# Retention and a routed MoE on one core: full-array transposes, whole-token products and state sums a step ahead

## The chip, the cores and the metric

The kernel runs on one core of a Trainium2 chip. Its time is the device time of one launch in microseconds (us); the time before is the median of three runs. Engines are named as in the profile: PE is TensorE's matmuls, PEld its weight loads, DVE is VectorE, ACT ScalarE, POOL GpSimd, and SP SyncE, which only issues DMAs here. Lines such as L354 are lines of the kernel before.

## The reference

A retention layer makes 3072 tokens of 512 numbers, and each token then goes through the one of eight experts that its logits choose.

```python
for t in range(S):                       # q, k, v: (4, 8, 768, 64)
    state = gamma * state + k[t] (x) v[t]          # per batch and head, 64x64
    y[t] = scale * q[t] @ state
x = y.transpose(0, 2, 1, 3).reshape(3072, 512)
logits = x @ w_gate;  e = argmax(logits)           # 8 experts
gate_w = softmax(logits)[e];  eom = sigmoid(x @ w_output_gate)[e]
out = gate_w * eom * (relu(x @ w1[e]) @ w2[e])     # w1: 512x1024, w2: 1024x512
```

## The kernel before

**Retention.** Each batch of 768 tokens is worked in chunks of 128, two chunks a step: twelve steps j (NP), three a batch. All eight heads go together, as four groups g of two (NG). Every product is a quarter of the PE array, 64x64, so that four independent products can stand in it. A step turns the queries and keys by products with the identity (`turn_q` L279 and `turn_k` L296, 32 products each, copied out of PSUM by ACT as qt and kt), makes the scores within blocks of 64 tokens (`scores`, 32), masks them on DVE (`masked`, am), multiplies them with the scaled values vs (`group`, into py), adds the keys' and values' products to the running state in the PSUM tile st (`group` also, alternating with the former), copies that state out four times (sx, L362) and reads it with the queries (`read`, L371, into py again, closed by a one-column DVE copy "seen", L378). DVE scales py into yt (L382). `tokens` (L394) turns yt back to tokens by products with idw, which holds the identity and the two gate matrices side by side, so that the logits come out with the tokens; ACT copies the result as xr (L398).

**Routing, two steps later.** `route1` and `gate` on DVE find the expert (oh, ef) and the gate value gt, `rows` (L449) multiplies the tokens by gt into rows, `count` (L460) counts tokens per expert on PE, `route2` works out each token's place, and `scatter` sends rows to the array srt in DRAM by POOL.

**Order.** The stage is scheduled by hand: every engine runs its instructions as the code calls them, in line. PSUM pairs 0, 1 and 2 (`pair(n)`) are passed from hand to hand, `free` says which is empty. SP loads three steps ahead (`load(j + 3)`) and brings the first weights in the last steps (`w_at`; `s_at` splits them into a high and a low part, whi and wlo, on ACT, DVE and POOL).

**Head and MoE.** The expert with most tokens after the fifth step (`choose`, pick, read into an SP register by values_load) gets its first 256 rows worked in the tail of the retention stage, as "head": stage 1, relu on ACT, the low part on DVE (L572), stage 2, transposes ot. Its products are handed out piece by piece by `run_head(n)`. After the last scatter DVE ranks the experts, pads srt, and works out n_odd, the number of rows that need the rare path. Then eight MoE passes: `load_x` (L805) on SP brings sorted rows, `prep_x` transposes and splits them (xt, xh L823, xw), stage 1 (L836), hh and hl (L840, L841), stage 2 (L855). The last pass turns its output by twelve full transposes (L881).

Of the kernel before, what the change touches and what calls it, by code (L numbers as in the profile page):

```python
# [31 lines left out]
def retention_moe_kernel(  # L32
# [157 lines left out]
    with ExitStack() as actx:  # L190
# [40 lines left out]
        gv = ac.tile([P, NC, H], F32, name="gv")  # L231
        gq = ac.tile([P, NPB, 2, 2, NG, 64], F32, name="gq")
        gc = ac.tile([P, NC, 2, NG], F32, name="gc")
        idw = ac.tile([P, NG, 2, 64 + 2 * E], F32, name="idw")
# [3 lines left out]
        for u in range(2):  # L238
            for r in range(2):
                h = r ^ u  # L240
                nc.scalar.dma_start(
                    gq[half(r), 0, u, 0],
                    dec_q[h:h + 1].rearrange("o (g t) -> o g t", g=NG)[:, :, half(u)].broadcast_to([64, NG, 64]))
        for u in range(2):
            for r in range(2):
                h = r ^ u
                nc.scalar.dma_start(gc[half(r), :, u],
                                    dec_c[h:h + 1].rearrange("o (c g) -> o c g", g=NG).broadcast_to([64, NC, NG]))
        load(1)
        for x, w in enumerate((w_gate, w_ogate)):  # L250
            wv = w.rearrange("(g r f) e -> r f g e", r=2, f=64)
            for u in range(2):
                for r in range(2):
                    nc.sync.dma_start(idw[half(r), :, u, 64 + x * E:64 + x * E + E], wv[r ^ u])
        load(2)

        def gq_rest(jj):
            for w in range(2):
                if jj or w:
                    nc.gpsimd.tensor_mul(gq[:, jj, :, w], gq[:, 0, :, 0],  # L260
                                         gc[:, 2 * jj + w].unsqueeze(3).broadcast_to([P, 2, NG, 64]))

        def prep_v(j):
            c = 2 * (j % NPB)
            vs[j] = ap.tile([P, 2, H, D], F32, name="vs", tag="vs", bufs=2)
# [3 lines left out]
        def mm64(out, o, ro, lhs, rhs, start=True, stop=True):  # L269
            nc.tensor.matmul(out, lhs, rhs, start=start, stop=stop, skip_group_check=True)  # L270

        def turn_q(j, n):
            p = pt["q", j] = pair(n, "pq")
            pv = p.rearrange("p w (g r m) -> p w g r m", g=NG, r=2)
            for g in range(NG):
                for r in range(2):
                    for w in range(2):
                        for hh in range(2):
                            nc.tensor.matmul(pv[half(hh), w, g, r], qn[j][half(w), 2 * g + hh, r], ident[half(w), half(w)],  # L279
                                             start=True, stop=True, skip_group_check=True)  # L280

        def copy_q(j):
            t = qt[j] = ap.tile([P, 2, NG, P], F32, name="qt", tag="qt", bufs=2)
            nc.scalar.copy(t.rearrange("p w g (m r) -> p (w g) r m", r=2),
                           pt.pop(("q", j)).rearrange("p w (g r m) -> p (w g) r m", g=NG, r=2))
            qn.pop(j)

        def turn_k(j, n, ws):
            if 0 in ws:
                pt["k", j] = pair(n, "pk")  # L290
            pv = pt["k", j].rearrange("p u (w g s) -> p u w g s", w=2, g=NG)
            for w in ws:
                for g in range(NG):
                    for u in range(2):
                        for hh in range(2):
                            nc.tensor.matmul(pv[half(hh), u, w, g], kn[j][half(u), w, 2 * g + hh], ident[half(u), half(u)],  # L296
                                             start=True, stop=True, skip_group_check=True)

        def copy_k(j):
            t = kt[j] = ap.tile([P, 2, 2, NG, 64], F32, name="kt", tag="kt", bufs=2)  # L300
            nc.scalar.copy(t.rearrange("p u w g s -> p (u w g s)"), pt.pop(("k", j)).rearrange("p u x -> p (u x)"))

        def scores(j, n):
            p = pt["s", j] = pair(n, "sc")
            pv = p.rearrange("p hh (w g t) -> p hh w g t", w=2, g=NG)
            for w in (1, 0):
                for g in range(NG):
                    for hh in range(2):
                        for u in range(2):
                            nc.tensor.matmul(pv[half(u), hh, w, g], kt[j][half(hh), u, w, g], qt[j][half(hh), w, g, half(u)],  # L310
                                             start=True, stop=True, skip_group_check=True)
            kt.pop(j)

        def masked(j):
            pv = pt.pop(("s", j)).rearrange("p hh (w g t) -> p hh w g t", w=2, g=NG)
            for w in range(2):
                a = am[j, w] = ap.tile([P, 2, NG, 64], F32, name="am", tag="am", bufs=2)
# [14 lines left out]
        def values(j, n):  # L332
            pt["y", j] = (pair(n, "py"), set())

        def group(j, w, u):

            c = 2 * (j % NPB) + w
            py = newest(j)
            x = 1 - u
            st_ops, av_ops = [], []  # L340
            for g in range(NG):
                for hh in range(2):
                    if not (c == NC - 1 and u == 1):
                        st_ops.append((st[half(hh), g], kn[j][half(u), w, 2 * g + hh], vs[j][half(u), w, 2 * g + hh],
                                       c == 0 and u == 0 and g == 0))
                    r = hh
                    h = r ^ x
                    av_ops.append((py[half(r), x, w, g], vs[j][half(x), w, 2 * g + h], am[j, w][half(x), h, g],
                                   begins(j, x, r)))
            for n in range(2 * NG):  # L350
                for ops in (av_ops, st_ops):
                    if ops:
                        o, l, m, s = ops[n]
                        nc.tensor.matmul(o, l, m, start=s, stop=True, skip_group_check=True)  # L354

        def copy_s(j, w, u):
# [3 lines left out]
            if j < NP and not (j % NPB == 0 and w == 0 and u == 0):  # L360
                t = sx[j, w, u] = ap.tile([P, NG, 64], F32, name="sx", tag="sx", bufs=6)
                nc.scalar.copy(t, st)  # L362

        def read(j, w):
            py = newest(j)
            for g in range(NG):
                for hh in range(2):
                    for r in range(2):
                        u = hh ^ r
                        if (j, w, u) in sx:  # L370
                            nc.tensor.matmul(py[half(r), u, w, g], sx[j, w, u][half(hh), g], qt[j][half(hh), w, g, half(u)],  # L371
                                             start=begins(j, u, r), stop=True, skip_group_check=True)
            first = (j, w, 0) not in sx
            sx.pop((j, w, 0), None), sx.pop((j, w, 1), None)
            if first:
                return
            t = sm.tile([P, 1], F32, name="seen", tag="seen")
            nc.vector.tensor_copy(t, py[:, 0, w, NG - 1, 63:64])  # L378

        def copy_y(j):  # L380
            t = yt[j] = ap.tile([P, 2, 2, NG, 64], F32, name="yt", tag="yt", bufs=2)
            nc.vector.tensor_tensor(out=t.rearrange("p u w g t -> p (u w g t)"), in0=pt.pop(("y", j))[0].rearrange("p u x -> p (u x)"),  # L382
                                    in1=gq[:, j % NPB].rearrange("p u w g t -> p (u w g t)"), op=ALU.mult)
            kn.pop(j), vs.pop(j), qt.pop(j), am.pop((j, 0)), am.pop((j, 1))

        X = 64 + 2 * E

        def tokens(j, w, n):
            p = pair(n, "px")
            pv = p[:, :, 0:NG * X].rearrange("p hh (g x) -> p hh g x", g=NG)  # L390
            for g in range(NG):
                for r in range(2):
                    for u in range(2):
                        nc.tensor.matmul(pv[half(u), r ^ u, g], yt[j][half(r), u, w, g], idw[half(r), g, u],  # L394
                                         start=True, stop=True, skip_group_check=True)
            if w == 0:
                xr[j] = ap.tile([P, 2, 2, NG, X], F32, name="xr", tag="xr", bufs=2)
            nc.scalar.copy(xr[j][:, w].rearrange("p hh g x -> p hh (g x)"), p[:, :, 0:NG * X])  # L398
            if w == 1:
                yt.pop(j)  # L400

        def route1(j):
            x8 = xr[j].rearrange("p w hh g x -> p w (hh g) x")
# [651 lines left out]
```

## Time and profile before

| | |
|---|---|
| median of three runs | 540.55 us (538.72 to 542.15) |
| profiled execution | 538.24 us, of it the span 536.5 us |
| PE busy | 427.9 us, 80% of the span |
| DVE, ACT, POOL busy | 265.5, 182.1, 172.1 us |
| mean granted clock of PE | 0.903 |
| prologue, loop of twelve steps | to about 24 us, to about 200 us |
| tail with head and ranking | to about 251 us |
| MoE passes | to the end |

The span is the profiled program on its engines; 1.74 us of the execution's time lie around it. Busy shares are means over stages that are held by different things: the MoE passes keep PE full, the loop does not. [...]

### The profile page before, as it was taken

The numbers are of one execution on the slowest core, as the hardware profiler recorded it, in microseconds if no ns is written. First come the engines' busy times: TensorE is split into PE (matmuls) and PEld (weight loads), VectorE is DVE, ScalarE is ACT, GpSimd is POOL, SyncE is SP. The second block draws the span as 40 slices with busy tenths as digits, with TensorE's granted clock in tenths as the row PEclk, the third lists the DMA queues.
The fourth block names the chain that finished last, engine by engine and source line by source line (L and its number), as shares of the span: only waits on it lengthen the run. The fifth ranks groups of instructions, "written<-read, shape, count | busy, mean of one in ns | idle before, by whom it ended". The sixth has DMA issues, their size and how long they took to land.

```text
span 536.5 us, 16878 instructions
## 1 busy us (share of the span) xinstructions
PE 427.9 (80%) x7027; PEld 409.1 (76%) x7027; DVE 265.5 (49%) x756; ACT 182.1 (34%) x356; POOL 172.1 (32%) x215
## 2 busy tenths in 40 slices
PE   5267676866777546493699999999999999999993
PEld 3256565766666545493699999999999999999992
DVE  1012354565456775714645745754756557566211
ACT  2023332333225442111344433533534444444111
POOL 0325122333334553300232203424424344242442
PEclk9588688798789977796889999999999999999998
DMA  6669996518811442105657538448467484563001
GB/s 123 137 122 222 209 248 162 123 44 213 226 43 50 125 152 81 61 22 157 120 177 204 150 107 198 143 129 216 146 166 193 147 210 149 157 183 96 30 27 60
DMA packets 130072, 74.16 MB, mean 138 GB/s; under 512 B 60213, under 2 KB 118585, under 8 KB 129984
## 3 DMA queue, kind: packets, MB, share of 16 engines
q1 hardware_dynamic: 121872, 59.43, 43.8%
q0 software_dynamic: 5280, 13.23, 7.2%
q8 instruction: 57, 0.93, 0.8%
q10 hardware_dynamic: 2832, 0.31, 0.5%
q14 instruction: 31, 0.25, 0.1%
HBM read 59.73 MB, written 13.70 MB: 137 GB/s over the span
## 4 chain that ended last, share of the span: by engine, by line
PE 64%; issue 13%; DVE 7%; SPq 5%; DMA 4%; POOL 3%; ACT 2%; ACTq 0%; POOLq 0%; DVEq 0%
PE a L855 21%; PE h L836 21%; PE py L354 4%; SPq L228 3%; PE pk L296 3%; POOL out_dram L177 3%; PE h L567 2%; PE sc L310 2%; PE px L394 2%; PE pq L279 2%; PE py L371 2%; PE st L354 2%; PE a L583 2%; DMA xl<-srt 2%; DVE wlo L172 2%
## 5 line engine op out<-in xcount | busy, mean ns | idle before, releaser
L177 POOL DMA_INDIRECT out_dram<-ot,idi x84 | 83.2, 991 | 155.9 <-ACT hh L840 126.1
L836 PE MATMUL h<-xh,whi 128*128 128x224 f32 (+7 forms) x256 | 87.0, 340 | 8.6 <-ACT xh L823 8.6
L855 PE MATMUL a<-hh,whi 128*128 128x224 f32 (+7 forms) x256 | 86.7, 339 | 4.3 <-ACT hh L840 4.3
L836 PE MATMUL h<-xw,whi 128*128 128x224 f32 (+7 forms) x256 | 87.0, 340 | 0.0
L836 PE MATMUL h<-xh,wlo 128*128 128x224 f32 (+7 forms) x256 | 86.8, 339 | 0.0
L855 PE MATMUL a<-hl,whi 128*128 128x224 f32 (+7 forms) x256 | 86.6, 338 | 0.1
L855 PE MATMUL a<-hh,wlo 128*128 128x224 f32 (+7 forms) x256 | 86.3, 337 | 0.0
L172 DVE TENSOR_TENSOR wlo<-raw,whi 128x512 fp32r<-128x512 f32 x64 | 47.4, 745 | 57.6 <-ACT whi L170 54.5
L841 DVE SCALAR_TENSOR_TENSOR hl<-h,hh 128x224 fp32r<-128x224 f32 (+7 forms) x64 | 34.9, 546 | 62.0 <-ACT hh L840 61.9
L170 ACT CAST whi<-raw 128x512 fp32r<-128x512 f32 x64 | 39.7, 620 | 63.9 <-PE a L855 62.4
L840 ACT ACTIVATE hh<-h 128x224 fp32r<-128x224 f32 (+7 forms) x64 | 31.0, 485 | 82.3 <-PE h L836 82.3
L836 PEld LDWEIGHTS h<-xh,whi 128*128 128x128 f32 x256 | 49.7, 194 | 9.0 <-ACT xh L823 8.8
L362 ACT COPY sx<-st 128x256 f32<-128x256 f32 x44 | 16.4, 372 | 113.4 <-PE st L354 113.4
L855 PEld LDWEIGHTS a<-hh,whi 128*128 128x128 f32 x256 | 49.0, 191 | 4.9 <-ACT hh L840 4.5
L491 POOL DMA_INDIRECT srt<-row,posi x24 | 24.1, 1005 | 82.9 <-DVE acc L485 63.5
L836 PEld LDWEIGHTS h<-xw,whi 128*128 128x128 f32 x256 | 49.6, 194 | 0.5
L836 PEld LDWEIGHTS h<-xh,wlo 128*128 128x128 f32 x256 | 49.6, 194 | 0.2
L855 PEld LDWEIGHTS a<-hl,whi 128*128 128x128 f32 x256 | 49.0, 191 | 0.8 <-DVE hl L841 0.4
L855 PEld LDWEIGHTS a<-hh,wlo 128*128 128x128 f32 x256 | 48.9, 191 | 0.5
L354 PE MATMUL py<-am,vs 64*64 64x64 f32 x768 | 41.4, 251 | 9.5 <-DVE seen L378 6.1
L354 PE MATMUL st<-vs,kn 64*64 64x64 f32 x704 | 38.3, 251 | 11.1 <-issue 11.1
L354 PEld LDWEIGHTS py<-am,vs 64*64 64x64 f32 x768 | 34.0, 159 | 12.8 <-DVE seen L378 8.1
(169 smaller groups left out, 706.1 us busy)
## 6 DMA issues: line engine op xcount, KB each, us to landing
raw<-in_moe_w_dram SPq DMA_DIRECT2D x128, 256.0 KB, 3.0
qn<-in_q_dram SPq DMA_DIRECT2D x12, 512.0 KB, 6.4
kn<-in_k_dram SPq DMA_DIRECT2D x24, 256.0 KB, 6.3
vn<-in_v_dram SPq DMA_DIRECT2D x24, 256.0 KB, 5.7
xl<-srt SPq DMA_DIRECT2D x12, 211.2 KB, 4.7
xl<-srt SPq DMA_DIRECT2D x12, 195.0 KB, 4.8
out_dram<-ot,idi POOLq DMA_INDIRECT x84, 2.7
xl<-srt SPq DMA_DIRECT2D x4, 227.5 KB, 7.4
```

What stands on the lines that cost most here:

```text
L170: nc.scalar.copy(hi[:, 0], raw[:, 0])
L172: nc.vector.tensor_sub(lo[:, 0], raw[:, 0], hi[:, 0].bitcast(F32))
L177: st = nc.gpsimd.indirect_dma_start(out=dst, out_offset=bass.IndirectOffsetOnAxis(ap=idx, axis=0), in_=src, in_offset=None, bounds_check=n ...
L228: nc.sync.dma_start(t[:, w], chunks(src, j)[:, w * P:(w + 1) * P].rearrange("h p d -> p h d"))
L296: nc.tensor.matmul(pv[half(hh), u, w, g], kn[j][half(u), w, 2 * g + hh], ident[half(u), half(u)], start=True, stop=True, skip_group_check= ...
L354: nc.tensor.matmul(o, l, m, start=s, stop=True, skip_group_check=True)
L362: nc.scalar.copy(t, st)
L491: ins = nc.gpsimd.indirect_dma_start(out=srt, out_offset=bass.IndirectOffsetOnAxis(ap=idx, axis=0), in_=src, in_offset=None, bounds_check= ...
L836: nc.tensor.matmul(ps[:, 0:C], l[:, 0, w], r[:, dc, 0:C], start=(n == 0), stop=(n == 3 * NDC - 1))
L840: relu = nc.scalar.activation(hh, ps[:, 0:C], AF.Relu)
L841: nc.vector.scalar_tensor_tensor(out=hl, in0=ps[:, 0:C], scalar=0.0, in1=hh.bitcast(F32), op0=ALU.max, op1=ALU.subtract)
L855: mm = nc.tensor.matmul(accs[d][:, 0:C], l[:, 1, w], r, start=(f == 0 and n == 0), stop=(f == NF - 1 and n == 2))
```

## The change

**Turns.** Keys and queries are turned by eight full 128x128 transposes each, two heads at a time, in place of 32 quarter products. For the queries DVE first separates even and odd tokens (`split_q`). **Outputs.** In odd groups the two heads' halves of py are swapped (`swap`), so that one product of 128x144 a group and chunk turns yt back and makes the logits: eight a step in place of 32. idw, gq and the decay factors are laid out for that; gq is prepared from gb and gc, and gab is loaded in rows of 24 numbers where gc was loaded four numbers at a time. **Order.** Turns are two steps ahead, the state sums one (`sums(j + 1, ...)`), alternating with values or scores through `issue`. **Engines.** The rows go from DVE to ACT, the seen copies go, the head's PSUM pair is another, the read of pick moves to step 7, and the rest of the head is called behind n_odd.

```diff
+                nc.scalar.dma_start(gab[half(r), x].rearrange("p c g -> p (c g)"),
+                                    dec_c[r ^ x:(r ^ x) + 1].broadcast_to([64, NC * NG]))
...
+        def split_q(j):
+            t = ap.tile([P, 2, H, D], F32, name="qr", tag="qr", bufs=1)
+            nc.vector.tensor_copy(t.rearrange("p r h d -> p h r d"), qn[j])
+            qn[j] = t
...
         def turn_q(j, n):
             p = pt["q", j] = pair(n, "pq")
+            for r in range(2):
                 for g in range(NG):
+                    nc.tensor.transpose(p[:, r, g * P:(g + 1) * P],
+                                        qn[j][:, r, 2 * g:2 * g + 2].rearrange("p h d -> p (h d)"), ident)
...
+        def turn_k(j, n):
+            p = pt["k", j] = pair(n, "pk")
+            for w in range(2):
+                for g in range(NG):
+                    nc.tensor.transpose(p[:, w, g * P:(g + 1) * P],
+                                        kn[j][:, w, 2 * g:2 * g + 2].rearrange("p h d -> p (h d)"), ident)
...
+        def issue(*lists):
+
+            for n in range(max(len(x) for x in lists)):
+                for x in lists:
+                    for o, l, m, s in x[n:n + 1]:
+                        nc.tensor.matmul(o, l, m, start=s, stop=True, skip_group_check=True)
...
+        def sums(j, w, u):
 
             c = 2 * (j % NPB) + w
+            if j >= NP or (c == NC - 1 and u == 1):
+                return []
+            return [(st[half(hh), g], kn[j][half(u), w, 2 * g + hh], vs[j][half(u), w, 2 * g + hh], c == 0 and u == 0 and g == 0)
+                    for g in range(NG) for hh in range(2)]
...
+        def tokens(j, n):
             p = pair(n, "px")
+            m = rt["misc", j] = ps_1.tile([P, 512], F32, name="misc", tag="misc")
+            for w in range(2):
+                for g in range(NG):
+                    nc.tensor.matmul(p[:, w, g * X:(g + 1) * X] if g < NG - 1 else m[:, w * X:(w + 1) * X],
+                                     yt[j][:, w, g].rearrange("p u t -> p (u t)"), idw[:, g], start=True, stop=True,
+                                     skip_group_check=True)
...
+        def copy_x(j):
+            xr[j] = ap.tile([P, 2, NG, X], F32, name="xr", tag="xr", bufs=2)
+            nc.scalar.copy(xr[j][:, :, 0:NG - 1].rearrange("p w g x -> p w (g x)"), pt.pop(("x", j))[:, :, 0:(NG - 1) * X])
+            nc.scalar.copy(xr[j][:, :, NG - 1], rt["misc", j][:, 0:2 * X].rearrange("p (w x) -> p w x", w=2))
...
-                    nc.vector.tensor_scalar(
...
+                    nc.scalar.activation(
...
+                        AF.Copy, scale=gt[:, w:w + 1])
...
+        w_at = {7: (0,), 8: (1,), 9: (2, 3), 10: (4, 5), 11: (6,)}
+        s_at = {8: (0,), 9: (1,), 10: (2, 3), 11: (4, 5)}
...
+            new_y(j, 0)
+            av = {(w, u): values(j, w, u) for w, u in ((0, 1), (1, 1), (1, 0), (0, 0))}
+            issue(av[0, 1], sums(j + 1, 0, 0))
+            copy_s(j + 1, 0, 1)
             if more:
+                split_q(j + 2)
             if j >= 2:
                 route1(j - 2)
+            issue(av[1, 0], av[1, 1])
+            issue(read(j, 0, 0), read(j, 1, 1))
+            issue(av[0, 0], sums(j + 1, 0, 1))
+            copy_s(j + 1, 1, 0)
+            if j >= 2:
                 gate(j - 2)
+                rows(j - 2)
+                count(j - 2, j - 2 in (PICK, EARLY))
             if more:
+                turn_k(j + 2, 1)
+                copy_k(j + 2)
+                turn_q(j + 2, 2)
+                copy_q(j + 2, 0)
...
+            sc = scores(j + 1, 1) if j + 1 < NP else [[], []]
+            issue(sums(j + 1, 1, 0), sc[1][0:8])
+            copy_s(j + 1, 1, 1)
+            if more:
+                copy_q(j + 2, 1)
...
+            issue(read(j, 0, 1), read(j, 1, 0))
             copy_y(j)
+            issue(sc[0][0:8], sc[1][8:16])
+            issue(sc[0][8:16], sums(j + 1, 1, 1))
+            copy_s(j + 1, 2, 0)
...
+            if j >= 1:
+                tokens(j - 1, 2)
+                copy_x(j - 1)
...
-        run_head(1000)
...
         nc.vector.tensor_add(n_odd, no, late)
+        run_head(1000)
```

The order of PE's instructions at the end of a step of the loop, before (py values and reads, st sums, px tokens, sc scores, pq the queries' turn; a row is a run of products):

```order
L354 MATMUL py<-am,vs 64x64
L354 MATMUL st<-vs,kn 64x64
L394 MATMUL px<-idw,yt 64x80 x16
L371 MATMUL py<-qt,sx 64x64 x16
L354 MATMUL py<-am,vs 64x64 x8
L310 MATMUL sc<-qt,kt 64x64 x32
L279 MATMUL pq<-ident,qn 64x64 x32
```

After, in the middle of a step, from the count to the first sums and scores of the next pair:

```order
L460 LDWEIGHTS tri_b
L460 MATMUL misc<-oh,tri_b 128x16
L461 LDWEIGHTS ones_b
L461 MATMUL misc<-acc,ones_b 128x16
L301 MATMUL pk<-ident,kn 128x128 x8
L286 MATMUL pq<-ident,qr 128x128 x8
L313 MATMUL st<-vs,kn 64x64
L313 MATMUL sc<-qt,kt 64x64
```

The turns are eight rows of 128x128 each behind the count, and scores alternate with sums in the place of standing alone.

ACT's instructions of one step before (ex and ez belong to the routing, xr are token copies, kt and qt the turned keys and queries):

```order
L415 ACTIVATE ex<-d_1513 128x16
L431 ACTIVATE ez<-z 128x2
L398 COPY xr<-px 128x640
L362 COPY sx<-st 128x256 x2
L301 COPY kt<-pk 128x1024
L398 COPY xr<-px 128x640
L362 COPY sx<-st 128x256 x2
L284 COPY qt<-pq 128x8x2x64
```

And after:

```order
L415 ACTIVATE ex<-d_1483 128x16
L368 COPY sx<-st 128x256
L431 ACTIVATE ez<-z 128x2
L449 ACTIVATE row<-xr,gt 128x2x128 x4
L306 COPY kt<-pk 128x1024
L292 COPY qt<-pq 128x512
L368 COPY sx<-st 128x256
L292 COPY qt<-pq 128x512
L368 COPY sx<-st 128x256
L400 COPY xr<-px 128x2x432
L401 COPY xr<-misc 128x2x144
```

Four rows stand between ez and the key copy, and both token copies come at the end of the step.

DVE in the tail, before, from the head's last two low parts to the first rows of the MoE stage is L572, four transposes L598, the chain L770 to L780 that ends in n_odd, and then idi. After, it is:

```order
L805 TENSOR_TENSOR no<-no,on 128x1
L806 TENSOR_TENSOR n_odd<-no,late 128x1
L574 SCALAR_TENSOR_TENSOR h_3727<-h_3105,h_3727 128x256
L574 SCALAR_TENSOR_TENSOR h_3754<-h_3105,h_3754 128x256
L844 CAST idi<-xl 128x7
L849 STREAM_TRANSPOSE xt<-xl 128x224 x2
L574 SCALAR_TENSOR_TENSOR h_3781<-h_3105,h_3781 128x256
L851 TENSOR_TENSOR xw<-xt,xh 128x224 x2
```

n_odd now stands ahead of the head's last low parts (h), and the rows' preparing (idi, xt, xw) stands between them.

## Rows read from the trace of the kernel before

**Rows 1.** Windows: length, busy us per engine (instructions), granted clock, DMA share, GB/s.
```profile
37.40:200.00 162.60, 110.84 (x4648) 100.79 (x4648) 83.66 (x353) 57.36 (x116) 56.63 (x86) 0.83 0.61 153
51.40:69.20 17.80, 12.61 (x451) 11.45 (x443) 7.28 (x33) 4.39 (x9) 6.15 (x33) 0.66 0.98 213
63.50:64.00 0.50, 0.50 (x28) 0.50 (x24) 0.43 (x5) 0.00 (x0) 0.00 (x0) 0.50 0.69 157
117.00:118.00 1.00, 1.00 (x64) 1.00 (x65) 0.86 (x4) 0.69 (x1) 0.00 (x0) 1.00 0.00 0
250.74:272.30 21.56, 17.11 (x101) 16.41 (x102) 12.01 (x26) 7.92 (x18) 4.18 (x4) 0.74 0.68 159
272.30:488.00 215.70, 215.70 (x1214) 213.70 (x1214) 127.58 (x230) 93.50 (x176) 74.85 (x76) 1.00 0.60 168
```

**Rows 2.** Waits of PE, 24 to 205 us: total, times, longest.
```profile
PE st L354 <- issue: 11.1, 5, 3.2
PE px L394 <- issue: 8.9, 5, 2.8
PE py L354 <- DVE seen L378: 6.1, 13, 1.8
```

**Rows 3.** Windows inside the loop, columns as in the first group.
```profile
105.90:109.40 3.50, 2.44 (x128) 2.18 (x128) 0.90 (x7) 1.53 (x3) 0.09 (x1) 1.00 0.02 5
109.40:112.90 3.50, 2.64 (x127) 2.36 (x128) 1.38 (x2) 0.82 (x2) 3.18 (x3) 1.00 0.41 156
...
sum 18.30, PE 12.81 PEld 11.61 DVE 10.01 ACT 7.31 POOL 6.89; mean PE 2.56 PEld 2.32 DVE 2.00 ACT 1.46 POOL 1.38
```

**Rows 4.** DMA queues, 105.9 to 124.2 us: packets, MB, share of 16 engines.
```profile
q8 instruction: 5, 0.08, 1.9%
```

**Rows 5.** Groups by line, 0 to 260 us: busy us, mean ns of one.
```profile
L398 ACT COPY xr<-px 128x640 f32<-128x640 f32 x24 | 16.7, 697 | 11.9 <-PE px L394 11.9
L362 ACT COPY sx<-st 128x256 f32<-128x256 f32 x44 | 16.4, 372 | 113.4 <-PE st L354 113.4
L449 DVE TENSOR_SCALAR row<-xr,gt 128x256 f32<-128x256 f32 x48 | 13.7, 350 | 0.2
L301 ACT COPY kt<-pk 128x1024 f32<-128x1024 f32 x12 | 12.2, 1017 | 0.0
L172 DVE TENSOR_TENSOR wlo<-raw,whi 128x512 fp32r<-128x512 f32 x9 | 9.7, 1106 | 4.2 <-ACT whi L170 4.2
L431 ACT ACTIVATE ez<-z 128x2 f32<-128x2 f32 x12 | 2.4, 203 | 3.9 <-DVE z L429 3.9
```

**Rows 6.** Timeline of PE near the end: start, us, instruction.
```profile
526.20 1.20 PE L881 MATMUL po<-ident,otl 128*128 128x128 f32 x9 [0.25 <-DVE otl L870]
```

**Rows 7.** Timeline of DVE, 198 to 205.4 us.
```profile
198.80 1.22 DVE L382 TENSOR_TENSOR yt<-py,gq 128x1024 f32<-128x1024 f32 x1 [0.78 <-PE py L354]
...
202.47 0.57 DVE L405 TENSOR_REDUCE lg<-xr 128x32 f32<-128x256 f32 x1
...
204.45 0.17 DVE L429 TENSOR_REDUCE z<-j 128x2 f32<-128x16 f32 x1
...
205.00 0.16 DVE L436 SCALAR_TENSOR_TENSOR den<-ez,se 128x2 f32<-128x2 f32 x1
205.20 0.17 DVE L438 RECIPROCAL gt<-den 128x2 f32<-128x2 f32 x1
```

**Rows 8.** DMA issues, 9 to 22 us: KB each, median us to landing.
```profile
kn<-in_k_dram SPq DMA_DIRECT2D x2, 256.0 KB, 15.1
```

**Rows 9.** The same of the whole page.
```profile
kn<-in_k_dram SPq DMA_DIRECT2D x24, 256.0 KB, 6.3
```

**Rows 10.** Waits of SP, 198 to 300 us.
```profile
SPq L805 <- DVE n_odd L780: 12.1, 1, 12.1
```

**Rows 11.** Waits of PE, 198 to 300 us.
```profile
PE h L836 <- ACT xh L823: 8.6, 1, 8.6
PE a L855 <- ACT hh L840: 4.3, 1, 4.3
```

More of the change, by code (lines that the diff above doesn't have):

```diff
@@ L272, in turn_q @@
         def turn_q(j, n):
             p = pt["q", j] = pair(n, "pq")
[L274 to L292, printed above, removed]
-                for g in range(NG):
[L294 to L297, printed above, removed]
@@ L303, in scores, with every @@
+        def issue(*lists):
[3 more added lines that the diff above has]
+                        nc.tensor.matmul(o, l, m, start=s, stop=True, skip_group_check=True)
+        def every(a, b):
+            return [x for ab in zip(a, b) for x in ab]
         def scores(j, n):
@@ L305, in scores @@
             pv = p.rearrange("p hh (w g t) -> p hh w g t", w=2, g=NG)
[L306 to L312, printed above, removed]
+            return [[(pv[half(u), hh, w, g], kt[j][half(hh), w, g, half(u)],
+                      qt[j][half(hh), g, w * P + 64 * u:w * P + 64 * u + 64], True)
+                     for w in range(2) for g in range(NG) for u in range(2)] for hh in range(2)]
         def masked(j):
@@ L330, in begins, with new_y, values @@
             return new
-        def values(j, n):
+        def new_y(j, n):
             pt["y", j] = (pair(n, "py"), set())
-        def group(j, w, u):
+        def sums(j, w, u):
             c = 2 * (j % NPB) + w
-            py = newest(j)
[L339 to L354, printed above, removed]
+            if j >= NP or (c == NC - 1 and u == 1):
+                return []
+            return [(st[half(hh), g], kn[j][half(u), w, 2 * g + hh], vs[j][half(u), w, 2 * g + hh], c == 0 and u == 0 and g == 0)
+                    for g in range(NG) for hh in range(2)]
+        def values(j, w, u):
+            py = newest(j)
+            return [(py[half(hh ^ swap(g)), u, w, g], vs[j][half(u), w, 2 * g + hh], am[j, w][half(u), hh, g],
+                     begins(j, u, hh ^ swap(g)))
+                    for g in range(NG) for hh in range(2)]
         def copy_s(j, w, u):
@@ L360, in copy_s, with read @@
             if j < NP and not (j % NPB == 0 and w == 0 and u == 0):
-                t = sx[j, w, u] = ap.tile([P, NG, 64], F32, name="sx", tag="sx", bufs=6)
+                t = sx[j, w, u] = ap.tile([P, NG, 64], F32, name="sx", tag="sx", bufs=9)
                 nc.scalar.copy(t, st)
-        def read(j, w):
+        def read(j, hh, u):
             py = newest(j)
[L366 to L378, printed above, removed]
+            return [(py[half(hh ^ swap(g)), u, w, g], sx[j, w, u][half(hh), g],
+                     qt[j][half(hh), g, w * P + 64 * u:w * P + 64 * u + 64], begins(j, u, hh ^ swap(g)))
+                    for w in range(2) if (j, w, u) in sx for g in range(NG)]
```

202 lines of the change are left out of this document (99 added, 103 removed).

## The prediction

> **What bounds the kernel now.** I read the stages by windows first, then TensorE's waits in the loop, then short windows inside a step. From 37.4 us on, where the second step begins, to the last y of the loop at 198.80 [rows 7] eleven steps take (198.8 - 37.4) / 11 = 14.7 us each. TensorE is busy for only 110.84 of 162.60 us of that stretch, at a mean granted clock of 0.83; DVE, the next, for 83.66 [rows 1]. The reader should look at what ends TensorE's waits: the longest are "issue", 11.1 us ahead of the state sums and 8.9 ahead of the token products; the wait for the vector engine's "seen" copy is 6.1 [rows 2]. "Issue" is no semaphore, so neither an engine nor a transfer is named. The short windows show what it is. With the clock at 1.00 and transfers nearly idle, TensorE takes 127 or 128 product records and as many weight-load records in 3.50 us, stops, and does so again; over one stretch it is 3.50, 3.50, 3.90, 3.80 and 3.60 us, mean 3.66, with 2.44 to 2.64 us of work in each (two of the five stand in [rows 3]). In the same 18.3 us the queue that carries instructions moved five packets, 0.08 MB [rows 4]: five blocks of 16 KB, one for each 256 records. So one block comes every 3.66 us, and **the loop is held by the supply of TensorE's instructions**, not by its arithmetic. A step's 224 quarter products are two passes each, 448 product and 448 load records, four a product, 896 in all: 3.5 blocks, 12.8 us at 3.66, near the 14.7 that a step takes; the rest is the lower clock and the waits for other engines.
>
> [...]
>
> **Fewer instructions.** A step after has 128 quarter products (sums 32, values 32, state reads 32, scores 32) at four records each, 512; sixteen full transposes, one product record and one load each (twelve transposes of the last pass are twelve records: nine of them stand in [rows 6]), 32; eight token products of two passes, 32; and four for the count: 580, or 2.27 blocks. That is 8.3 us at 3.66 a block. In the slowest stretch, 51.4 to 69.2, 451 product records took 17.80 us [rows 1], waits and a clock of 0.66 included: 5.05 us for each 128, which gives 11.5. Since 8.3 to 11.5 lies below 14.7 in any case, the question is what is late next.
>
> **The chain that is late next.** The order keeps every engine in line, and ACT now has the rows ahead of the key copy. So a step has this ring: token products, copy of them on ACT, routing and gate on DVE, rows on ACT, key copy on ACT, the scores on TensorE (they take the PSUM pair from which the keys are copied, and so wait for that copy), and the next token products. The pieces:
> - token products, a shape that the trace does not have. The nearest row is nine transposes in 1.20 us, 0.133 each [rows 6]; eight products of two passes at 0.133 are 2.1 us. At half the clock they would be 4.2. I take 2.1.
> - copy of the tokens in two parts: the 256-wide copy is 372 ns, the 640-wide 697 [rows 5], so 0.85 ns an element and 0.16 to begin; 864 and 288 wide give 0.89 + 0.40 = 1.3.
> - routing and gate: 202.47 to 205.37 in the tail, where nothing else holds them, 2.9 [rows 7].
> - four rows: 350 ns each on DVE; on ACT as the 372 ns copy of the same size [rows 5], 1.5.
> - key copy: 1.0 [rows 5].
> - sums, scores and reads behind it: 64 products, 128 records. At clock 1.00 TensorE takes 64 records in 1.00 us, at 0.50 it takes 28 in half a us [rows 1]: 2.0 us, or 2.3 at half.
> - crossings between engines: z ends at 204.62, den begins at 205.00, and between them lies only ACT's ez of 203 ns [rows 5, 7]: 0.09 a crossing, eight of them 0.7.
>
> Sum: 2.1 + 1.3 + 2.9 + 1.5 + 1.0 + 2.0 + 0.7 = **11.5 us** a step, above the supply's 8.3. TensorE's other work (half the quarter products, 2.0, the transposes, 16 x 0.133 = 2.1, the count) lies beside the 6.7 us in which the ring is on ACT and DVE; if that cover goes, 4 us come in. The clock stood at 0.83 over the loop [rows 1]; that is two thirds of the time at 1.00 and one at 0.50, and a third of the 2.4 us that half the clock adds (4.2 + 2.3 in place of 2.1 + 2.0) is 0.8. I take 12.0, of 12.3; 10.5 as the low end (part of the ring overlapped, 1.0) and 14.0 with half the clock throughout (the transposes' longer time still fits beside the 6.7).
>
> The new split of q on DVE costs about one pass over 1024 elements, 1.0 us like the key copy, up to 2.0 if its order of reading costs double; it stands ahead of the routing and needs a load begun a step earlier. Its cover is the token products and their copy, 3.4 us; if that goes, the ring is 1.0 to 2.0 longer, which the ends hold. The seen copies and the rows leave DVE, which is not late in the ring apart from the routing: nothing. The sums a step ahead take the state copies off the path of the reads, and with the seen copies the 6.1 us go; both lie in the 14.7 that the ring replaces. Loads need 1.57 MB a step; with DMA at 0.98 the rate was 213 GB/s [rows 1], 7.4 us, below 12. SP's read of the chosen expert now stands behind the loads of step 7, so no load waits for it.
>
> **Start.** The four loads of gc, 1536 pieces of 16 bytes, become 256 of 96 bytes, and the gate weights' pieces halve. Beside them the first key chunks landed 15.1 us after issue [rows 8], where the median of all is 6.3 [rows 9]. The gain is up to 15.1 - 6.3 = 8.8 us, at least nothing. Against it, what stands ahead of step 1 now holds one pair's turns and sums more, and three splits of q, each with a load to wait for; I put that at 8, most of a supply-bound step. I take step 1 at 36.5 (37.4 before); ends 32 and 46.
>
> **Loop end.** Step 1 has no routing: 10 us, by the supply. Steps 2 to 9: 8 x 12.0 = 96. The last two have no turns (9.5 each) but the splits of the weights, 1.1 us a piece on DVE [rows 5], and with those of steps 8 and 9 some 4.7 on the path: 23.7. 36.5 + 10 + 96 + 23.7 = 166 instead of 198.8: **-33**. Ends: 8 x 10.5 gives -45; 2.0 more in each of eleven steps gives -11.
>
> **Tail.** Before, the load of the first MoE rows waited 12.1 us for n_odd [rows 10], which was queued on DVE behind the head's last products; TensorE then waited 8.6 us for the cast rows and 4.3 for hh, which stood behind the next rows' casts [rows 11]. After, n_odd is ahead of the head, so rows load while the head runs, and DVE's and ACT's preparing of them stands between the head's steps, which I estimate from their places in the order at 3 us for the head, none to 6. Routing of the last pair is 1.5 later (rows on ACT, weight casts ahead). So: 8.6 - 3 - 1.5 = 4 and the second wait with its half-speed stretch (21.56 us for 17.11 of work at 0.74 [rows 1]) another 4 to 8. I take **-10**, ends -2 and -13. From 272.3 on TensorE is busy without a gap, 215.70 of 215.70 [rows 1]; nothing there changes.
>
> **Sum.** 538.24 (span 536.5 and 1.74 around it) - 33 - 10 = 495. This execution is 2.3 below the median of the runs shown, so for that median 497.
>
> **Rivals.**
> A, the clock falls. [...] For: it is at 0.50 at 63.5 us, and the loop's mean is 0.83 [rows 1]; TensorE will stand idle for 2 to 3 us a step while the ring is on ACT and DVE. Against: the nine transposes of the end keep 0.133 [rows 6], and stops of 1 us at 1.00 did not lower it [rows 3]. Eleven steps 2.0 longer give 497 + 22 = 519. [...] No row shows a long run of transposes.
> B, the stops are not a matter of the number of instructions (one stop for so many products or so much time, say). For: no row has another number of instructions a product. Against: the five packets [rows 4]. Steps stay at 14.7: 8 x 2.7 = 22 is lost, about 8 more in the last steps: 527.
> C, slower than before. ACT's rows stand ahead of the key copy and of two state copies, and wait for DVE's gate, which waits for q's split and that for a load: if the ring takes in the rest of TensorE's step too (4 us), the split (2.0) and a late load, a step is 11.5 + 4 + 2 + 2 = 19.5: 497 + 8 x 7.5 = 557. It decides from 497 + 8 x (s - 12) = 540.55, s = 17.4 us a step. For: transfers were at 0.98 in 51 to 69 us [rows 1]. Against: a load has a whole step of slack, and DVE is idle for half of the loop.
>
> **How the numbers follow.** My forecast (485 to 512) 0.70, A 0.13, B 0.08, C 0.05, better than 485 (ring of 10.5, early start, tail -13: 482) 0.04. The range 482 to 521 takes in the ends of the ring and A; B and C are left out. One per cent, 5.4 us, is about what a measurement of this kernel can tell from no change. Faster by over 1% are the forecast, the better case, A and most of B, 0.91; within 1% 0.04; slower 0.05.
>
> **What would show it.** Right: the loop's TensorE records per step near 290 instead of 448; blocks of 256 records still 3.5 to 4.2 us where TensorE runs on; "issue" far below 11.1 and 8.9 us; in its place TensorE waiting for the key copy and ACT for gt; the last y near 166; the first MoE load without n_odd. Wrong: issue waits as long as now at fewer records (B), a clock near 0.6 in the loop (A), DVE's split waiting for q (C), or a ring that overlaps more than I allow.

## The result, and the profile after

The kernel after takes 501.98 us (median of 4 runs, 498.35 to 505.92), the kernel before 540.35: ratio 0.9273, 95% interval 0.9199 to 0.9348, 7.3% faster. The ratio leaves out runs more than 1.5% above the fastest of their kernel, so it is not quite the quotient of the medians. Forecast were 497, range 482 to 521. The profiled execution took 504.32 us, of it the span 502.5; before 538.24, so 33.9 less.

The windows of after, columns as in [rows 1]; the first reaches from the first y of the loop to the last, the next seven are single steps, then the last step, the tail, and a stretch of the MoE passes:

```profile
32.40:168.90 136.50, 101.54 (x2963) 92.50 (x2952) 77.84 (x307) 69.04 (x155) 56.40 (x86) 0.89 0.69 170
42.90:55.50 12.60, 10.04 (x289) 9.35 (x282) 8.13 (x29) 6.22 (x15) 6.30 (x32) 0.86 0.96 207
55.50:67.00 11.50, 9.06 (x286) 7.94 (x280) 6.74 (x29) 6.64 (x16) 5.68 (x6) 1.00 1.13 247
67.00:81.90 14.90, 10.76 (x296) 9.69 (x291) 6.21 (x28) 7.09 (x17) 4.96 (x7) 0.84 1.04 246
93.70:104.40 10.70, 8.76 (x290) 8.12 (x283) 7.21 (x35) 6.49 (x16) 4.16 (x6) 1.00 0.22 72
104.40:115.30 10.90, 8.91 (x308) 8.19 (x301) 6.21 (x29) 6.80 (x16) 4.37 (x6) 1.00 0.96 245
115.30:126.40 11.10, 8.92 (x286) 8.06 (x281) 6.14 (x28) 6.22 (x15) 4.20 (x6) 1.00 0.45 151
126.40:140.60 14.20, 10.56 (x294) 9.65 (x289) 9.16 (x35) 7.57 (x18) 5.93 (x7) 0.88 0.22 76
150.90:168.90 18.00, 8.87 (x195) 8.12 (x187) 11.59 (x37) 6.61 (x14) 8.08 (x9) 0.69 0.36 119
168.90:223.00 54.10, 37.79 (x230) 36.25 (x231) 24.85 (x113) 14.94 (x36) 13.72 (x16) 0.78 0.38 105
250.00:460.00 210.00, 210.00 (x1154) 208.13 (x1153) 124.67 (x224) 89.81 (x169) 71.44 (x72) 1.00 0.59 163
```

A step now holds about 290 product records and as many loads, as forecast, in place of some 450 [rows 1]. The steps from the second y (42.88) to the tenth (140.59) take 12.2 us, forecast 12.0. PE's waits, 0 to 260 us, columns as in [rows 2]:

```profile
PE misc L460 <- DVE oh L419: 17.9, 7, 7.3
PE h L569 <- DVE h L574: 10.6, 3, 5.1
PE sc L313 <- ACT kt L306: 7.1, 6, 1.5
PE st L313 <- issue: 2.4, 2, 1.9
PE py L313 <- issue: 1.9, 2, 1.1
```

"Issue" was 11.1 and 8.9 us ahead of single products [rows 2]; it is 2.4 and 1.9. All rows of PE's waits that are put down to issue, added up from the first y to the last, come to 37.5 us before and 8.8 after. In place of these PE waits for the routing (oh) and for the key copy (kt). Timelines of DVE show the first and the last y, which stood at 32.44 and at 198.80 [rows 7] before:

```profile
32.39 1.23 DVE L379 TENSOR_TENSOR yt<-py,gq 128x1024 f32<-128x1024 f32 x1 [5.13 <-PE py L313]
...
168.89 1.23 DVE L379 TENSOR_TENSOR yt<-py,gq 128x1024 f32<-128x1024 f32 x1 [1.25 <-PE py L313]
```

So the loop gave 198.80 - 168.89 = 29.9 us (forecast 33), and all that follows it (536.5 - 198.8 = 337.7, now 502.5 - 168.9 = 333.6) gave 4.1 (forecast 10).

The last y is not the same place in the work, though. Before, the token products of the last pair but one stand ahead of it; after, they stand behind it, and so does all that follows from them. PE's timeline, and then DVE's with the start of that pair's routing:

```profile
170.83 1.65 PE L392 MATMUL px<-idw,yt 128*128 128x144 f32 x6
```
```profile
176.56 0.35 DVE L405 TENSOR_REDUCE lg<-xr 128x32 f32<-128x128 f32 x1
```

Before, this routing begins at 202.47 [rows 7], 3.7 us behind the last y, now 7.7 behind it. Measured to there, the first part gave 25.9 us and the rest 8.1.

### The profile page after: what moved, and what is told of

Same layout as the page of the kernel before. It is cut to its first block, busy times and chain, and to the rows that moved or that the text cites. A ratio compares the mean times of both kernels' runs of the same rounds, so it can differ in the third digit from the quotient of the medians.

```text
span 502.5 us, 13022 instructions
## 1 busy us (share of the span) xinstructions
PE 430.8 (86%) x5107; PEld 411.6 (82%) x5107; DVE 260.0 (52%) x709; ACT 203.5 (41%) x416; POOL 170.5 (34%) x214
## 4 chain that ended last, share of the span: by engine, by line
PE 50%; issue 8%; DMA 5%; DVE 5%; ACT 3%; POOL 3%; SPq 0%; POOLq 0%; ACTq 0%; DVEq 0%
PE h L863 22%; PE a L882 22%; DMA srt<-row,posi 5%; POOL out_dram L177 3%; PE px L392 2%; PE a L585 1%; ACT row L449 1%; PE sc L313 1%; PE h L569 1%; ACT whi L170 1%; PE py L313 1%; DVE wlo L172 1%; DMA xl<-srt 1%; DVE xw L851 0%; ACT kt L306 0%
## 5 line engine op out<-in xcount | busy, mean ns | idle before, releaser
L863 PE MATMUL h<-xh,whi 128*128 128x224 f32 (+7 forms) x256 | 85.7, 335 | 1.6 <-issue 1.6
L863 PE MATMUL h<-xh,wlo 128*128 128x224 f32 (+7 forms) x256 | 85.7, 335 | 0.0
L863 PE MATMUL h<-xw,whi 128*128 128x224 f32 (+7 forms) x256 | 85.6, 334 | 0.0
L172 DVE TENSOR_TENSOR wlo<-raw,whi 128x512 fp32r<-128x512 f32 x64 | 45.3, 707 | 70.9 <-ACT whi L170 67.9
L170 ACT CAST whi<-raw 128x512 fp32r<-128x512 f32 x64 | 39.7, 621 | 63.8 <-PE a L882 63.8
L863 PEld LDWEIGHTS h<-xh,whi 128*128 128x128 f32 x256 | 48.6, 190 | 2.0 <-issue 1.8
L863 PEld LDWEIGHTS h<-xw,whi 128*128 128x128 f32 x256 | 48.5, 190 | 0.3
L863 PEld LDWEIGHTS h<-xh,wlo 128*128 128x128 f32 x256 | 48.5, 189 | 0.2
L491 POOL DMA_INDIRECT srt<-row,posi x24 | 24.0, 1002 | 46.5 <-ACT row L449 24.5
L171 ACT CAST whi<-raw 128x512 fp32r<-128x512 f32 x64 | 39.5, 618 | 0.0
L313 PEld LDWEIGHTS st<-vs,kn 64*64 64x64 f32 x704 | 30.3, 147 | 11.0 <-issue 5.7
L173 DVE TENSOR_TENSOR wlo<-raw,whi 128x512 fp32r<-128x512 f32 x56 | 38.3, 684 | 0.0
```

Of the source, the lines that this page charges most:

```text
L170: nc.scalar.copy(hi[:, 0], raw[:, 0])
L171: nc.scalar.copy(perm(hi), r2)
L172: nc.vector.tensor_sub(lo[:, 0], raw[:, 0], hi[:, 0].bitcast(F32))
L173: (nc.gpsimd if s < NF else nc.vector).tensor_sub(perm(lo), r2, perm(hi).bitcast(F32))
L491: ins = nc.gpsimd.indirect_dma_start(out=srt, out_offset=bass.IndirectOffsetOnAxis(ap=idx, axis=0), in_=src, in_offset=None, bounds_check= ...
L863: nc.tensor.matmul(ps[:, 0:C], l[:, 0, w], r[:, dc, 0:C], start=(n == 0), stop=(n == 3 * NDC - 1))
```

## The experiments

The runs came in three groups of four, e1 to e4, e5 to e8 and e9 to e12. Each group was run on a chip of its own, with its own runs of before beside it, 539.6, 548.9 and 538.88 us; ratios are to those, and between groups only ratios are compared.

**Records against work: e1 and e2.** Both add products of zeros behind the count, into columns that nothing reads.

```diff
+            if j < LAST - 1:
+                for _ in range(64):
+                    nc.tensor.matmul(misc[0:64, 128:144], wz[0:64, 0:64], wz[0:64, 0:16], start=True, stop=True, skip_group_check=True)
```

e2 has `range(10)` and 128x128 products with 384 columns.

> The kernel before, with 64 tiny products more (64x64 against 16 columns of zeros, bf16, into unused columns of the count's PSUM tile) behind the count of each of the steps 2 to 11: one product and one load record each, 128 records a step, half a block. Their work is at most some 2 us a step. If the loop is held by the supply of TensorE's instructions at 3.66 to 4.2 us for 256 records: 10 x 0.5 x 3.66 to 4.2 = 18 to 21 us more, about 559. If the stops are not about the number of instructions but TensorE's time counts: up to 20 more here, and as much in the run with the large products. If neither counts: no change.

> The kernel before, with 10 large products more (128x128 against 384 columns of zeros, bf16) in the same place: 20 records a step, but TensorE's work of about 1.6 to 2 us a step, the same as that of the 64 tiny ones or more. If supply holds the loop: 10 x 20 / 256 x 3.9 = 3 us more at most, 540 to 544, since TensorE's work lies in the stops. If TensorE's time counts: 16 to 20 more, about 558.

e1 took 566.65 us, ratio 1.0514 (1.0440 to 1.0588), 27 us more; e2 547.82, 1.0164 (1.0104 to 1.0223), 8 more. PE's timelines, e1 first:

```profile
61.77 3.42 PE L464 MATMUL misc<-wz 64*64 64x16 bf16 x61
115.14 2.64 PE L464 MATMUL misc<-wz 64*64 64x16 bf16 x61
```
```profile
61.94 3.33 PE L464 MATMUL misc<-wz 128*128 128x384 bf16 x10
113.26 1.79 PE L464 MATMUL misc<-wz 128*128 128x384 bf16 x10
```

The loop's windows from the first y to the last, before, e1 and e2, columns as in [rows 1]:

```profile
32.40:198.80 166.40, 111.82 (x4711) 101.63 (x4700) 84.88 (x354) 56.53 (x115) 55.69 (x85) 0.84 0.62 154
32.40:225.60 193.20, 146.85 (x5343) 138.65 (x5335) 85.11 (x354) 57.24 (x117) 55.88 (x86) 0.73 0.55 133
33.10:205.50 172.40, 124.95 (x4807) 103.90 (x4799) 83.89 (x354) 56.55 (x116) 54.32 (x84) 0.86 0.59 147
```

The large products, 1.8 to 3.3 us of PE a step, 24.2 in all, cost the loop 0.67 us a step (its last y is at 205.50 in place of 198.80): most of that time fits into the stops, and the loop's issue waits fall from 37.5 to 29.9 us (24 to 205 us). The tiny ones, 2.3 to 3.6 us a step, 32.6 in all, cost 2.7 a step (last y at 225.60). The 108 records between the two make 2.0 us a step, 4.7 for 256 where 3.66 to 4.2 were expected. But the issue waits of e1's loop fall too, to 27.4: what it has more is TensorE's busy time (146.85 against 111.82), that of the tiny products themselves, at a clock of 0.73. So the pair shows that TensorE's own time in the stops costs little, and e1 fits a price for each record, but by itself it doesn't show one: that tiny products simply take long would do as well. The next two runs take records away.

**Fewer records in the old order: e3 and e5.**

```diff
+            p = pt["k", j]
             for w in ws:
                 for g in range(NG):
-                    for u in range(2):
-                        for hh in range(2):
-                            nc.tensor.matmul(pv[half(hh), u, w, g], kn[j][half(u), w, 2 * g + hh], ident[half(u), half(u)],
-                                             start=True, stop=True, skip_group_check=True)
+                    nc.tensor.transpose(p[:, w, g * P:(g + 1) * P],
+                                        kn[j][:, w, 2 * g:2 * g + 2].rearrange("p h d -> p (h d)"), ident)
```

e5 does the same for the queries, with `split_q(j + 2)` called ahead of the second `read`.

> The kernel before, with the keys alone turned by eight full transposes in place of 32 quarter products; order, queries, outputs and sums stay. 128 records become 16 in each of twelve turns, while the work is alike (8 x 0.116 against 128 x 0.015 us at most). Supply: 12 x 112 / 256 x 3.66 to 4.2 = 19 to 22 us less, about 520. Rival, that the new order of the stage made the gain and not the number of records: within 3 us of before.

> The run with the keys' full transposes, and the queries' too, in the order of the kernel before: DVE splits q a step ahead, ACT copies the turned queries as in the kernel after. 112 records a step fewer again, 672 in place of 896. By supply at 3.66 to 4.2 us a block another 19 to 22 us, about 504; at the price that the keys alone had (14.7 us for 112 records a step) 510. Rival, that the order made the gain of the change: no more than the keys gave, 522 to 527.

PE's groups of the keys' turns, 0 to 260 us, before and then e3 (total us, mean ns of one):

```profile
L296 PE MATMUL pk<-ident,kn 64*64 64x64 f32 x768 | 21.0, 245 | 8.4 <-issue 5.3 <-ACT qt L284 1.8 <-DMA kn<-in_k_dram 1.3
L294 PE MATMUL pk<-ident,kn 128*128 128x128 f32 x96 | 21.1, 358 | 1.9 <-DMA kn<-in_k_dram 1.9
```

e3: 524.95 us, ratio 0.9749 (0.9677 to 0.9821), 15 less; e5: 527.02 beside a before of 548.9, 0.9592 (0.9544 to 0.9639), 1.6% or some 9 us more. In e3 the turns keep TensorE as long as before, with an eighth of the records, and the issue waits of the loop fall from 37.5 to 30.8 us: it is the count and not TensorE's time. (Products and weight loads go one to one, 7027 of each before, 5107 after, 4148 and 4139 in e3's loop, so which of them counts stays open.) Both signs are those of supply, both sizes below its full price (19 to 22 each): the freed time goes in part into other waits. The waits of PE in e11 (below), which has both turns in the old order, 24 to 190 us:

```profile
PE py L356 <- DVE seen L380: 14.5, 15, 3.9
...
PE py L373 <- issue: 4.6, 3, 2.7
```

Issue is small now, and the "seen" copies, 6.1 in [rows 2], are the longest wait. In e5 I had called the second split of q in the prologue ahead of the first mask, where DVE waits 17.41 us for a load with all that stands behind; e11 has it later. e5's first y comes at 36.48 us, 4 later than before.

**The first loads: e4.**

```diff
+                nc.scalar.dma_start(gab[half(r), u].rearrange("p c g -> p (c g)"),
+                                    dec_c[h:h + 1].broadcast_to([64, NC * NG]))
```

> The kernel before, with the decay factors of the chunks loaded as 256 pieces of 96 bytes in place of 1536 of 16 bytes, and nothing else. If these pieces held the first loads back: loads behind them some 8 us earlier, and the end of the loop earlier by up to 8.8 us, since the first steps wait for loads; about 533. Rival: the first steps are held by the supply of instructions too, and the earlier loads are only waiting longer: no change.

528.94 us, ratio 0.9821 (0.9758 to 0.9885), 10.7 less; all its y come 7 to 9 us earlier, the first at 24.44, the last at 191.38. DMA issues from 0 to 22 us, before and then e4:

```profile
gc<-in_dec_c_dram ACTq DMA_DIRECT2D x4, 6.0 KB, 12.2
```
```profile
gab<-in_dec_c_dram ACTq DMA_DIRECT2D x4, 6.0 KB, 5.4
```

The pieces themselves land in 5.4 us in place of 12.2, and SP's queue, which they are not on, comes to the gate weights at 15.76 us in place of 24.18.

**The ring: e6 and e7.** e6 puts the keys' quarter products back into the kernel after (their copy then sorts them); e7 moves ACT's key copy ahead of the rows:

```diff
-                rows(j - 2)
                 count(j - 2, j - 2 in (PICK, EARLY))
             if more:
                 turn_k(j + 2, 1)
                 copy_k(j + 2)
+            if j >= 2:
+                rows(j - 2)
+            if more:
                 turn_q(j + 2, 2)
```

> The kernel after with the keys turned by 32 quarter products again (their copy sorts them): 692 records a step in place of 580, 2.7 blocks, 9.9 to 11.3 us. If the ring through routing, rows and key copy holds the loop now at 10.8 to 12.4 us a step: 0 to 4 us more, 502 to 506. If supply still holds it: 19 to 22 more, about 523.

> The kernel after with ACT copying the turned keys ahead of the four rows in place of behind them, nothing else. If that ring holds the loop: 1.5 to 1.7 us less in each of the eight steps that have rows and keys, about 12 less, 490. If the loop is held by something else (supply, loads, DVE): no change, 500 to 504.

e6: 0.9301 (0.9240 to 0.9363) of its before. The kernel after had 0.9273, and 0.9255 in e9: 112 records more a step cost no more than can be measured, where the same 112 were worth 2.5% in the kernel before. Supply no longer holds the loop as a whole, though single stops are left. e7: 0.9194 (0.9135 to 0.9254), about 0.7% less than after, some 4 us where 12 were expected; the intervals overlap, so by itself it is open. In its waits (24 to 190 us) the scores no longer wait for kt; the routing is what is left:

```profile
PE misc L460 <- DVE oh L419: 19.0, 9, 7.3
PE sc L313 <- issue: 4.2, 8, 0.9
```

**The tail: e8 and e10.** e8 calls `run_head(1000)` ahead of n_odd again in the kernel after. e10 is the kernel before with one line more:

```diff
+        spare = ac.tile([P, 2048], F32, name="spare")
```

> The kernel after with the rest of the head called ahead of n_odd again, as in the kernel before. The tail's term of the prediction (10 us less) rests on this: about 10 more, 512. The rival, from the trace of after, where the first MoE load waits for the padded rows to land instead and the tail is no shorter: within 4, 498 to 506.

> The kernel before with one more tile of 8 KB a partition that nothing uses, which moves the buffers of the MoE stage to other addresses: the first load of rows then no longer waits for the head's last instructions and n_odd, while head and n_odd stand as before. If the wait was one for memory: the load starts some 12 us earlier, the 8.6 us of TensorE go and about 4 to 8 of the second cold stretch: 8 to 12 us less, 529 to 532 where before is 540. If it was the order of n_odd behind the head, as the prediction has it: no change.

e8: 0.9240 (0.9194 to 0.9287), the same as after within what can be measured. e10: 526.24 us, 0.9764 (0.9724 to 0.9804), 12.6 less, from a tile that nothing touches. SP's waits, 150 to 300 us, in e8 and then in e10:

```profile
SPq L832 <- DMA srt<-zrow,si: 7.5, 1, 7.5
```
```profile
SPq L806 <- DMA srt<-zrow,si: 7.5, 1, 7.5
```

In neither does the load wait for n_odd [rows 10], though in both n_odd stands behind the head as it did before; both wait for rows, the padded ones last, to land. SP's timeline shows the first load's issue, before and then in e10:

```profile
245.38 1.97 SPq L805 DMA_DIRECT2D xl<-srt  x4
```
```profile
233.80 1.99 SPq L806 DMA_DIRECT2D xl<-srt  x4
```

It starts 11.6 us earlier with nothing but addresses moved, so the wait was for memory and not for the order. Which memory, no run shows; the likely reading is that the first buffer of rows lay where the retention stage had kept tiles that the head and the n_odd chain were still using. e10's first MoE product no longer waits for the cast rows (8.6 us in [rows 11]); PE's timeline:

```profile
247.38 0.34 PE L837 MATMUL h<-xh,whi 128*128 128x224 f32 x1 [1.58 <-issue]
```

It comes at 247.38, 3.4 earlier than at 250.74 before, with the last y 0.45 later; from there to the end of the span it is 276.5 in place of 285.8: 9.3 us are the second wait and the slow stretch behind it (before, the granted clock is 0.74 over the first 21.56 us [rows 1]: 0.50 from 250.74 to 255.11, where products start 0.21 us apart, and 1.00 from 255.28 to 261.08, where they start 0.11 apart; in e10 they start 0.11 apart from 247.56 to 253.14).

**After once more, the old order with four edits, and a faster one: e9, e11, e12.** e11 is the kernel before with e3's and e5's turns (the second split behind the first mask), e4's layout and e10's tile. e12 is the kernel after with e7's and e8's moves, the splits ahead of the tokens, and the head's rows prepared a step later, behind the last y:

```diff
+            for s in s_at.get(j, ()):
+                split_weights(s)
+            if j == EARLY + 4:
+                head_prep(0)
+                head_prep(1)
             if j >= 1:
                 tokens(j - 1, 2)
                 copy_x(j - 1)
-            for s in s_at.get(j, ()):
-                split_weights(s)
...
+        split_weights(6)
         tokens(LAST, e2)
         copy_x(LAST)
-        split_weights(6)
```

> The kernel after once more, unchanged, beside the next three on the same chip, as their base: 0.927 of before.

> The kernel before in its own order, with four edits: full transposes for the keys and the queries, the decay factors in 256 pieces, and the unused tile. Sums stay in their step, token products stay quarters, rows stay on DVE. If instructions, first loads and the memory wait are what the change gained by: 15 + 9 + 11 + 9 = 44 less at most, with some of it lost to other waits 500 to 508, within 2% of the kernel after. If the order and the token products matter: 515 or more.

> The kernel after with the weights' splits called ahead of the token products in place of behind their copy (steps 8 to 11 and the tail), the head's rows prepared a step later, the keys copied ahead of the rows, and the rest of the head ahead of n_odd. By the trace of after, the routing of the last steps no longer waits for the splits: 5.5 us less in the last step, 3 and 2 in the tail, 0 to 5 by the head's order, 0 to 4 by the keys: 10 to 16 less than the kernel after, 0.90 of before. If the last steps are held by something else: as after.

e9: 498.78 us, 0.9255 (0.9213 to 0.9298). e11: 496.06, 0.9199 (0.9164 to 0.9235): the old order with four edits is as fast as the kernel after. The single gains, 15 + 9 + 10.7 + 12.6 = 47, come to 42.8 together. So what the change has beyond these four (the new order, whole-token products, sums a step ahead, rows on ACT) gave no net gain that these runs can tell; none of it was taken out alone. e12: **479.71 us**, 0.8872 (0.8833 to 0.8911), 19 us faster than the kernel after beside it. What it took away is seen in after's last step, in DVE's timeline:

```profile
157.77 0.69 DVE L172 TENSOR_TENSOR wlo<-raw,whi 128x512 fp32r<-128x512 f32 x1 [3.92 <-ACT whi L170]
158.81 1.35 DVE L172 TENSOR_TENSOR wlo<-raw,whi 128x512 fp32r<-128x512 f32 x1 [0.34 <-ACT whi L170]
160.08 1.22 DVE L553 CAST idx<-xl 128x8 int32<-128x8 f32 x1
161.34 0.17 DVE L554 TENSOR_TENSOR idx<-idx,no 128x8 int32<-128x8 int32 x1
161.42 1.42 DVE L558 STREAM_TRANSPOSE xt<-xl 128x256 f32<-128x256 f32 x4
162.76 0.32 DVE L405 TENSOR_REDUCE lg<-xr 128x32 f32<-128x128 f32 x1
```

The tokens' copy was done at 157.2, the routing that needs it begins at 162.76, behind two splits and the head's rows; PE's count waits 7.3 us for it and the last y with it. In e12, the same waits, 24 to 190 us:

```profile
PE misc L460 <- DVE oh L419: 5.9, 5, 2.4
```

It is 16.4 in e9. e12's last y is at 149.13, e9's at 165.12: 16 of the 19 us are in the loop. How they divide among its four edits no run shows; from y to y three steps in the middle take 10.2 to 10.6 us, against 10.8 to 11.3 in e9, and the last four 41.9 against 52.8: 10.9 of the 16 us lie there, and another 4 in one early step.

## Why the prediction was right, point by point

**Supply held the loop: right.** e3 and e5 bear it out in the old order, e2, where TensorE's time in the stops cost little (0.67 us a step for 2.4 us of products), and e6 (0.9301 of its before, after 0.9273), where the same records cost nothing that can be measured once the loop is held by something else. e1 fits, but its added time is its products' own. The price of a block as I used it (3.66 us off the path for every 256 records) was too high for a part of the change: e3 and e5 gave 15 and 9 us for 112 records each, not 19 to 22, since "seen" waits took the place of part of it. For the whole change that did not matter, because the forecast replaced the step by the next bound and did not subtract blocks.

**The ring: right, piece by piece.** ACT's timeline of after, one step:

```profile
96.53 0.88 ACT L400 COPY xr<-px 128x864 f32<-128x864 f32 x1 [1.52 <-PE px L392]
97.30 0.40 ACT L401 COPY xr<-misc 128x288 f32<-128x288 f32 x1
...
100.60 1.71 ACT L449 ACTIVATE row<-xr,gt 128x256 f32<-128x256 f32 x4 [0.67 <-DVE jr L475]
102.21 0.99 ACT L306 COPY kt<-pk 128x1024 f32<-128x1024 f32 x1
```

and PE's:

```profile
94.51 1.00 PE L392 MATMUL px<-idw,yt 128*128 128x144 f32 x6
...
99.57 1.06 PE L301 MATMUL pk<-ident,kn 128*128 128x128 f32 x8
...
103.25 0.27 PE L313 MATMUL sc<-qt,kt 64*64 64x64 f32 x1 [1.50 <-ACT kt L306]
...
105.27 1.00 PE L392 MATMUL px<-idw,yt 128*128 128x144 f32 x6
```

Token products 94.51 to 96.6 (2.1, forecast 2.1), copies to 97.7 (1.2; 1.3), routing, gate and crossings to 100.60 (2.9; 2.9 and crossings), rows 1.7 (1.5), keys 1.0 (1.0), scores and the rest to the next tokens at 105.27 (2.0; 2.0): 10.8 us around, forecast 11.5. Not all of it was as hard as I took it: e7 and e12 take the rows' 1.7 us out and the step shortens by some 0.5 only (from the second y to the tenth 13.0 us a step in e7, 13.6 in e8, which has after's loop on the same chip).

**The mean step: right in part by luck.** The 12.2 on the mean agree with 12.0, but not through a slow clock, on which I had put the difference: three steps of 10.7 to 11.1, at a clock of 1.00, stand beside longer ones. Five steps to 93.7 us have a DMA share of 0.96 to 1.13, and the one from 67.0 to 81.9 takes 14.9 us. TensorE waits for no load in it; its long waits are two stops, at a clock of 0.84:

```profile
69.40 0.27 PE L313 MATMUL sc<-qt,kt 64*64 64x64 f32 x1 [1.64 <-issue]
...
75.60 0.27 PE L313 MATMUL st<-vs,kn 64*64 64x64 f32 x1 [1.92 <-issue]
```

Of the 8.8 us of issue waits that are left in the loop, 7.1 lie ahead of 82 us. That busy transfers make the stops longer is a guess: the step from 104.4 has a share of 0.96 and takes 10.9. The step from 126.4 takes 14.2 for another reason, that of the last one: a split of weights and the split of q stand ahead of the routing on DVE, and the count waits 2.7 us for it.

**Start: right in the sum.** The first y stands where it was; e4 shows that the earlier loads were worth 8 us at that place, which the longer prologue takes up. The second y, where the forecast has 36.5 + 10 = 46.5, came at 42.88.

**Last steps: 18.0 us in the last one** where I had 9.5 and part of 4.7; the last two take 28.3, forecast 23.7. So the end of the loop, 168.9 for 166, is near because the 3.6 us gained up to the second y and the 4.6 lost in the last two steps nearly cancel. The splits were counted, but their place ahead of the routing on DVE was not followed: e12.

**Tail: the term that failed.** The step was "n_odd is ahead of the head, so rows load while the head runs". The rows do load while the head runs (issued from 206.88 us on, the head's last transposes start at 221.46), but e8 and e10 show that the order of n_odd has no part in it; what lies where in memory does. The second half (the second wait and its slow stretch, 4 to 8) came: from the first MoE product at 223.0 to the end it is 279.5 in place of 285.8. The first half did not: from last y to first MoE product it is 54.1, and 51.9 before. DVE's transposes at the end of the head, before and then after:

```profile
242.22 1.44 DVE L598 STREAM_TRANSPOSE ot<-a 128x256 f32<-128x256 f32 x4 [2.03 <-PE a L583]
```
```profile
221.46 1.44 DVE L600 STREAM_TRANSPOSE ot<-a 128x256 f32<-128x256 f32 x4 [2.02 <-PE a L585]
```

The first MoE product stands 1.5 us behind them, 8.5 before: 7.0 of the 8.6 are gone, as forecast. But the end of the head stands 52.6 us behind the last y, 43.4 before: 9.2 more. The routing of the last pair begins 0.8 of that later (forecast 1.5); the rest, 8.3, lies between it and the end of the head (36.7 us, 28.4 before), where I had 3. About 4 of the 8.3 are the price of calling the head behind n_odd: e8 has 32.3 there and 48.9 for the whole stretch, though the timed runs can't tell e8 from after. The other 4 e8 has too, and no run shows what they are. PE's wait for h behind the routing chain, 10.6 us, is not what is new: it was 9.3.

**Rivals.** A, the clock falls: it did not; it is 0.89 over the loop, and 1.00 in steps with sixteen transposes each. Eight of them take 1.06 us, 0.13 each, at a granted clock of 1.00, with other products before and behind them; how a long run of transposes alone would fare no run shows. B fell with e3 and e5. C: steps reach 17.4 only once, in the last step.

## What to carry to other kernels

Look at a wait called "issue" in windows of whole instruction blocks: if an engine stops after equal numbers of instructions whatever it computes (here 127 or 128 products in 3.50 us [rows 3]), count its instructions, and replace small products by few large ones, until the next ring binds. Then look for what is cheaper still: here an unused tile that moved a buffer was worth 12.6 us and a load in larger pieces 10.7, together more than half of what the whole change gave, with a few lines. Work that is off the path in one step (here the splits) belongs behind the routing in an engine's order, or ahead of where that engine would wait anyway.

## What the runs showed of the hardware that was not expected

In e1 TensorE is busier than before (146.85 of 193.2 us of the loop against 111.82 of 166.4) and yet its mean granted clock is lower, 0.73 against 0.84; in e2, with 24.2 us of large products in place of 32.6 of tiny ones, it is 0.86. Loads of 1536 pieces of 16 bytes held not only themselves (12.2 us to landing, 5.4 in e4 with 256 pieces) but the loads on another queue, by 8 us (its gate weights at 24.18 us, 15.76 in e4).
